# K~ by pairs, h in two parts, rows from two engines and the scan's profiled durations in a planned attention and feed-forward kernel

## The chip, the cores and the metric

The kernel runs on one core of one Trainium2 chip. The metric is device microseconds of one execution. A run of each kernel consists of several timed executions and one profiled one; where ratios are given, they are the mean time of one kernel's fast runs over the mean time of the other's fast runs of the same rounds, so they are not quite the ratio of the medians that are quoted beside them.

## The reference

Two blocks follow each other. The first is a gated linear recurrence with a complex decay; the second is a feed-forward layer with a squared relu. Cut to what matters:

```python
# q, k, v, a_re, a_im: (batch 4, heads 8, seq 768, head_dim 48), fp32
a = (a_re, a_im) * min(|a|, 0.999) / (|a| + 1e-6)
for t in range(S):                      # S complex, 48 x 48 per head
    S = a[t] * S  (complex)
    S.re += outer(k[t], v[t])
    y[t] = q[t] @ S.re
x = y, heads side by side               # 3072 tokens x 384
h = x @ w_in                            # 384 -> 2048
out = maximum(h, 0) ** 2 @ w_out        # 2048 -> 384
```

## The kernel before

The work is cut into 8 units: 4 batches times 2 halves of 384 rows. In each unit VectorE computes running products of the decay (the "scan", which leaves them in `e` and `x`), TensorE transposes them back (`tot`, `bk`), multiplies them into q and k (`P`, only in units 0 and 1, the "early" ones), and goes through four pairs of heads: `tq` transposes, `sa` scores, `kv` states, `ypair` the mix of both. Each pair's result `yt` is moved by DMA into the rows `xT`. Then come 16 products `h` (768 matmul records for all units, 0.32 us each, two for each matmul call) and the products `o`. Weights arrive as raw words and VectorE converts them (`w`), with ScalarE's help (`lower`, tile `raw`).

The program sets the order on every engine. The kernel registers steps with an engine, a planned cost, a lag, a rank and dependencies, and a small list scheduler lays them out once, while the program is built:

```python
step(key, engine, cost, rank, deps, fn, lag=None, bank=None, until=None)

def lay_out():                          # cut
    while ready:
        # for every engine: the earliest ready step, rank breaks near ties
        ...
        free[engine] = t + cost         # the plan's clock, not the chip's
        done[key] = t + cost + lag
```

So a planned cost changes no work; it moves the place of later steps in an engine's list. The parts that the change touches:

```python
# the scan's planned cost (10 parts on VectorE in every unit)
sizes = [96] * 3 + [48, 45, 42, 36, 24, 45]
costs = [dve_cost(2 * m, 2 * m, m, m) for m in sizes] + [dve_cost(*[279] * 6)]
# dve_cost(*ns) is the sum of 80 + int(1.04 * n)
...
def rows(z, i):         # K~ through memory, half a unit (2 pairs, 576 KB) at a time
    if i == 0:
        nc.gpsimd.dma_start(out=<rows in memory>, in_=<all of u["K", z]>)
    else:
        nc.gpsimd.dma_start(out=<KC>, in_=<rows in memory, read another way>)
...
def place():            # a pair's rows of xT
    for h in range(2):
        ...
            nc.sync.dma_start(out=u["xT"][...], in_=u["yt", i][...])
...
def hidden(f):          # one block of h
    ps = u["h", f] = dp.tile([C, L], F32, name="h", tag="d")
    for m in range(NM):                 # NM = 3
        nc.tensor.matmul(ps, lhsT=w1[:, f, m], rhs=u["xT"][:, m], ...)
...
step(("h", n, f), "PE", 1940, ..., [("xT", n, i) for i in range(NP)] + ...)
```

## Time and profile before

| | before |
|---|---|
| time, median of 3 | 777.3 us (776.74 to 778.57) |
| span of the profiled execution | 776.3 us |
| h of unit 0 starts | 90.27 us |
| unit 1's scan ends on VectorE | 155.3 us |
| h of unit 1 starts | 191.85 us |
| from there to the end | 584.45 us |

The last two rows cut the span in two: a first part, in which the early units start up, and a second part, in which the units follow each other.

GpSimd's order of time (start, duration, engine, line, transfer; in brackets what it waited for before):

```profile
72.51 1.52 POOL L658 DMA_DIRECT2D raw<-in_moe_w_in_dram  x2 [3.46 <-DVE w L683]
74.03 0.76 POOL L1100 DMA_DIRECT2D KC<-rows  x1
```

The read back stands behind two weight fetches, which wait for VectorE.

### The profile page before, as it was taken

Reading aid. Unit: us, or ns where it says so; the run is one execution under the profiler, and the core shown is the slowest. Engines: PE = TensorE matmul, PEld = TensorE weight load, DVE = VectorE, ACT = ScalarE, POOL = GpSimd, SP = SyncE. Lnnn points to the kernel's source line nnn. Section 1 sums busy time; section 2 is a strip of 40 time slices with the busy share of each in tenths; the row PEclk is TensorE's granted clock in tenths of the full one; section 3 lists DMA queues with packets and bytes.
Section 4 is the critical chain, followed back from the end, with each engine's and each line's share of the span. In section 5 each row is a group of like instructions: output and inputs, shape, how many; then the busy total and the mean of one; then the engine's idle time right before and its main releaser. Section 6 shows DMA issues by size and latency. Waiting matters only on the chain.

```text
span 776.3 us, 9918 instructions
## 1 busy us (share of the span) xinstructions
PE 709.7 (91%) x3538; PEld 474.8 (61%) x3538; DVE 503.3 (65%) x1184; ACT 409.8 (53%) x754; POOL 107.2 (14%) x157
## 2 busy tenths in 40 slices
PE   0249699998899999999999999999999999999997
PEld 0138555577568657766866676676577555555553
DVE  4789888879796797769667988967954660000000
ACT  5638187346868538772867378686154303502510
POOL 5002100031031103102110401310022420000000
PEclk9999699999899999999999999999999999999999
DMA  9517462043134207203520522331052870000000
GB/s 278 168 30 238 141 206 77 21 154 109 35 118 141 58 20 230 54 3 111 176 51 1 178 82 56 125 121 38 15 193 90 292 238 11 2 11 21 0 11 24
DMA packets 39067, 76.24 MB, mean 98 GB/s; under 512 B 10752, under 2 KB 25216, under 8 KB 39008
## 3 DMA queue, kind: packets, MB, share of 16 engines
q0 software_dynamic: 14208, 53.88, 21.7%
q1 hardware_dynamic: 24800, 21.64, 9.2%
q8 instruction: 30, 0.49, 0.3%
q14 instruction: 29, 0.24, 0.1%
HBM read 56.62 MB, written 14.16 MB: 91 GB/s over the span
## 4 chain that ended last, share of the span: by engine, by line
PE 68%; DVE 21%; ACT 3%; DMA 3%; issue 2%; SPq 0%; POOL 0%; ACTq 0%; DVEq 0%
PE h L1280 24%; PE o L1297 23%; DVE fa L982 5%; PE sa L1186 5%; PE tq L1173 4%; PE kv L1200 3%; PE ypair L1222 3%; DVE e L989 3%; PE P L1081 2%; PE ypair L1227 2%; DMA KC<-rows 2%; DVE fa L987 1%; ACT fa L808 1%; DVE e L990 1%; DMA xT<-yt 1%
## 5 line engine op out<-in xcount | busy, mean ns | idle before, releaser
L1280 PE MATMUL h<-xT,w 128*128 128x384 f32 x768 | 261.1, 495 | 6.5 <-DMA xT<-yt 6.5
L1297 PE MATMUL o<-w,g 128*128 128x384 f32 x768 | 254.5, 487 | 0.0
L1280 PEld LDWEIGHTS h<-xT,w 128*128 128x128 f32 x768 | 144.9, 193 | 101.4 <-issue 8.4
L1297 PEld LDWEIGHTS o<-w,g 128*128 128x128 f32 x768 | 143.5, 190 | 94.1 <-issue 0.7
L1287 ACT ACTIVATE g<-h 128x384 f32<-128x384 f32 x128 | 62.5, 488 | 93.4 <-PE h L1280 93.3
L1178 ACT COPY QKT<-tq 96x512 f32<-96x512 f32 x96 | 76.2, 871 | 34.2 <-PE tq L1173 33.5
L1302 ACT COPY ot<-o 128x384 f32<-128x384 f32 x24 | 11.5, 479 | 122.9 <-PE o L1297 121.3
L1290 ACT ACTIVATE g<-g 128x384 f32<-128x384 f32 x128 | 67.0, 523 | 3.5
L1186 PE MATMUL sa<-QKT 96*128 96x128 f32 x384 | 53.8, 282 | 1.5 <-ACT QKT L1178 0.9
L1186 PEld LDWEIGHTS sa<-QKT 96*128 96x128 f32 x384 | 47.7, 191 | 7.9 <-ACT QKT L1178 1.9
L1173 PE MATMUL tq<-ident,QK 128*96 128x128 f32 x384 | 50.8, 273 | 0.4 <-DVE QK L1087 0.4
L1192 DVE TENSOR_TENSOR A<-sa,mask 128x384 f32<-128x384 f32 x64 | 35.2, 552 | 22.5 <-PE sa L1186 21.6
L982 DVE TENSOR_TENSOR fa<-e 128x192 f32<-128x192 f32 (+6 forms) x152 | 48.3, 358 | 2.0
L1173 PEld LDWEIGHTS tq<-ident,QK 128*96 128x96 f32 x384 | 42.4, 126 | 10.2 <-issue 6.4
L808 ACT ACTIVATE fa<-fb 128x576 f32<-128x576 f32 x64 | 41.3, 675 | 6.3 <-DVE fb L816 3.5
L935 PE MATMUL tot<-ident,last 128*128 128x128 f32 x72 | 12.6, 306 | 31.1 <-ACT last L861 27.3
L805 DVE TENSOR_TENSOR fb<-fa 128x576 f32<-128x576 f32 x32 | 24.1, 755 | 25.8 <-ACT fa L800 13.6
L1222 PE MATMUL ypair<-A,v 128*48 128x128 f32 x384 | 37.7, 287 | 2.4 <-ACT yt L1232 1.9
L762 POOL DMA_DIRECT2D a<-in_a_re_dram x12 | 9.0, 753 | 209.3 <-issue 99.3
L1200 PE MATMUL kv<-v,KC 128*96 128x48 f32 x320 | 32.7, 254 | 2.9 <-DMA KC<-rows 2.9
L1200 PEld LDWEIGHTS kv<-v,KC 128*96 128x96 f32 x320 | 31.7, 173 | 5.5 <-DMA KC<-rows 2.8
L1087 DVE TENSOR_TENSOR QK<-qk,fa 128x576 f32<-128x576 f32 x48 | 33.1, 755 | 0.0
(105 smaller groups left out, 828.6 us busy)
## 6 DMA issues: line engine op xcount, KB each, us to landing
rows<-QK POOLq DMA_DIRECT2D x16, 576.0 KB, 4.0
raw<-in_moe_w_in_dram POOLq DMA_DIRECT2D x16, 384.0 KB, 7.7
raw<-in_moe_w_out_dram SPq DMA_DIRECT2D x16, 384.0 KB, 3.7
look<-in_moe_w_in_dram POOLq DMA_DIRECT2D x16, 384.0 KB, 4.6
look<-in_moe_w_out_dram POOLq DMA_DIRECT2D x16, 384.0 KB, 4.6
KC<-rows POOLq DMA_DIRECT2D x8, 576.0 KB, 5.4
out_dram<-ot SPq DMA_DIRECT2D x24, 192.0 KB, 1.9
xT<-yt SPq DMA_DIRECT2D x48, 72.0 KB, 2.8
```

The costliest lines, as they stand in the source:

```text
L808: act.activation(out=parts(z)[dst], in_=parts(z)[src], func=func, **kw)
L982: dve.tensor_tensor(out=t, in0=x, in1=y[:, j].unsqueeze(1).to_broadcast(shape), op=ALU.mult)
L1173: nc.tensor.transpose(ps[:, 2 * j + h], src, ident)
L1178: act.copy(out=u["T", i].rearrange("r z (p c) -> r c z p", c=W)[:, c], in_=u["tq", i, c])
L1186: nc.tensor.matmul(sa[:, j], lhsT=T[:, 2 + h, ts(j, C)], rhs=T[:, h, ts(j, C)], start=True, stop=True)
L1192: dve.tensor_tensor(out=u["A", i][:, h], in0=u["sa", i, h], in1=mask3, op=ALU.mult)
L1200: nc.tensor.matmul(ps[:, j, h], lhsT=u["KC", hh // HH][:, j, hh % HH], rhs=u["v"][:, j, hh], start=True, stop=True)
L1222: nc.tensor.matmul(ypair[64 * h:64 * h + D, ts(j, C)], lhsT=u["v"][:, j, 2 * i + h], rhs=A[:, h, j], start=True, stop=S_j is None)
L1280: nc.tensor.matmul(ps, lhsT=w1[:, f, m], rhs=u["xT"][:, m], start=(m == 0), stop=(m == NM - 1))
L1287: act.activation(out=t, in_=u["h", f], func=AF.Relu)
L1290: act.activation(out=u["g", f], in_=u["g", f], func=AF.Square)
L1297: nc.tensor.matmul(u["o", c], lhsT=u["g", f][:, ts(c, C)], rhs=w2[:, f], start=(f == 0), stop=(f == NF - 1))
```

## The change

Its intent has four parts: in units 0 and 1 send K~ through memory pair by pair, with the last product stage `P` ordered by pairs too; split the first three blocks of h so that two thirds of each need no last rows of xT; let ScalarE issue half of the last rows in those units; and give the plan the scan's durations as profiled. One more edit comes with it: the q and k loads of unit 1 are now planned behind the last read back of K~ of unit 0. (Some planned lags and ranks move too: of the first `a` loads, of the K~ transfers, of the rows and of h.) Cut to its core:

```diff
@@ loads
-                        if name == "a" else [("ap", n - 1, z)],
+                        if name == "a" else [("ap", n - 1, z)]
+                        + ([("KC", 0, 1, NP - 1)] if n == 1 else []),
@@ scan
-        sizes = [96] * 3 + [48, 45, 42, 36, 24, 45]
-        costs = [dve_cost(2 * m, 2 * m, m, m) for m in sizes] + [dve_cost(*[279] * 6)]
+        costs = [1475] * 3 + [1010, 980, 940, 880, 760, 970, 2300]
@@ K~ through memory
+        def pairs_of(z):
+            of_z = range(z * NP // 2, (z + 1) * NP // 2)
+            return list(of_z) if early else [of_z]
...
+            for i in pairs_of(z):
+                ... one "rows" and one "KC" transfer for each entry
@@ the last rows of xT
+        def aside(h):
+            return n < 2 and i == NP - 1 and h == 1
...
+                (nc.scalar if aside(h) else nc.sync).dma_start(
@@ h in two parts
+            apart = f < BANKS["d"]
+            if apart:
+                step(("h0", n, f), "PE", 1290, ..., lambda f=f: hidden(f, range(NM - 1)), ...)
+            step(("h", n, f), "PE", 650 if apart else 1940, ...
+                 lambda f=f, apart=apart: hidden(f, [NM - 1] if apart else range(NM)), ...)
```

More of the change, by code (lines that the diff above doesn't have):

```diff
@@ L775, in chain_steps @@
                         [("f", n - 1, z, i, r) for i in range(2) for r in range(2)]
-                        if name == "a" else [("ap", n - 1, z)],
+                        if name == "a" else [("ap", n - 1, z)]
+                        + ([("KC", 0, 1, NP - 1)] if n == 1 else []),
                         lambda name=name, z=z, j=j: load(name, z, j),
-                        lag=(3300 + 1500 * z if name == "a" else 8000) if n == 0 else 6000)
+                        lag=(3300 + 2500 * z if name == "a" else 8000) if n == 0 else 6000)
         for j in range(W):
@@ L1088, in apply, with rows @@
                               in0=u["qk", z][:, j, hi], in1=p, op=ALU.mult)
-        def rows(z, i):
-            if i == 0:
+        def rows(z, i, back):
+            if ("rows", z) not in u:
                 u["rows", z] = dram.tile([L, HH * R], F32, name="rows", tag=f"rows{z}")
+            m = HH // len(pairs_of(z)) * R
+            e = slice(i % (HH * R // m) * m, (i % (HH * R // m) + 1) * m)
+            if not back:
                 nc.gpsimd.dma_start(
-                    out=u["rows", z].rearrange("(p c) e -> p (c e)", c=W),
-                    in_=u["K", z].rearrange("p c h e -> p (c h e)"))
-            else:
-                kc = u["KC", z] = nat.tile([C, NM, HH, R], F32, name="KC", tag=f"KC{z}")
-                m = NM - u["half"]
-                nc.gpsimd.dma_start(
-                    out=kc[:, 0:m].rearrange("p j h e -> p j (h e)"),
-                    in_=u["rows", z].rearrange("(j p) e -> p j e", p=C)[:, 0:m])
+                    out=u["rows", z].rearrange("(p c) e -> p c e", c=W)[:, :, e],
+                    in_=u["K", z].rearrange("p c h e -> p c (h e)")[:, :, e])
+                return
+            if ("KC", z) not in u:
+                u["KC", z] = nat.tile([C, NM, HH, R], F32, name="KC", tag=f"KC{z}")
+            j = NM - u["half"]
+            nc.gpsimd.dma_start(
+                out=u["KC", z][:, 0:j].rearrange("p j h e -> p j (h e)")[:, :, e],
+                in_=u["rows", z].rearrange("(j p) e -> p j e", p=C)[:, 0:j, e])
+        def pairs_of(z):
+            of_z = range(z * NP // 2, (z + 1) * NP // 2)
+            return list(of_z) if early else [of_z]
         for z in range(2):
@@ L1106, in chain_steps @@
             was_read = [("tq", n - 1, i, c) for i in of_z for c in range(W)] + [
-                ("rows", n - 1, z)]
+                ("rows", n - 1, z, i) for i in of_z]
             add(("ov", n, z), "DVE", D1, [("xn", n, 2), ("rest", n, z), ("kk", n, z)],
@@ L1114, in chain_steps @@
             done = []
-            for r in range(2):
-                made = [("f", n, z, 0, r), ("f", n, z, 1, 1 - r)]
-                if early:
-                    for i in range(2):
-                        P = ("P", n, z, r, i)
-                        qk = [("QK", n, z, j, r, i) for j in (1, 0)]
-                        add(P, "PE", 970, made + [("ov", n, z)] + was_read, lambda z=z, r=r, i=i: join_pe(z, r, i),
-                            rank=-3000 if z == 0 else -1950 + 40 * n, bank="sc", until=qk[1])
-                        for j, key in zip((1, 0), qk):
-                            add(key, "DVE", 410, [P, qk[0] if j == 0 else P], lambda z=z, j=j, r=r, i=i: apply(z, j, r, i))
-                            done.append(key)
-                else:
-                    add(("join", n, z, r), "DVE", D1, made,
-                        lambda z=z, r=r: join(z, r))
+            for i, r in ((i, r) for i in range(2) for r in range(2)) if early else ():
+                P = ("P", n, z, r, i)
+                qk = [("QK", n, z, j, r, i) for j in (1, 0)]
+                add(P, "PE", 970, [("f", n, z, 0, r), ("f", n, z, 1, 1 - r), ("ov", n, z)]
+                    + was_read, lambda z=z, r=r, i=i: join_pe(z, r, i),
+                    rank=-3000 if z == 0 else -1950 + 40 * n, bank="sc", until=qk[1])
+                for j, key in zip((1, 0), qk):
+                    add(key, "DVE", 410, [P, qk[0] if j == 0 else P],
+                        lambda z=z, j=j, r=r, i=i: apply(z, j, r, i))
+                    done.append(key)
+            for r in () if early else range(2):
+                add(("join", n, z, r), "DVE", D1, [("f", n, z, 0, r), ("f", n, z, 1, 1 - r)],
+                    lambda z=z, r=r: join(z, r))
             if not early:
@@ L1136, in chain_steps @@
             add(("ap", n, z), "DVE", 0, done, lambda: None)
-            for i, (name, lag) in enumerate((("rows", 4800), ("KC", 5200))):
-                add((name, n, z), "POOL", 750,
-                    [x for x in done if x[3] == 1] + [("rows", n, z) if i else ("KC", n - 1, z)]
-                    + ([("kv", n - 1, x) for x in of_z] if i else []),
-                    lambda z=z, i=i: rows(z, i), rank=-100, lag=lag)
+            for i in pairs_of(z):
+                whole_z = not early
+                keys = [x for x in done if x[3] == 1 and (whole_z or x[5] == i % 2)]
+                pairs = of_z if whole_z else [i]
+                for name, lag, deps in (
+                        ("rows", 4800 if whole_z else 3800,
+                         keys + [("KC", n - 1, z, x) for x in of_z]),
+                        ("KC", 5200 if whole_z else 4200,
+                         [("rows", n, z, pairs[0])] + [("kv", n - 1, x) for x in of_z])):
+                    add((name, n, z, pairs[0]), "POOL", 750, deps,
+                        lambda z=z, i=pairs[0], name=name: rows(z, i, name == "KC"),
+                        rank=-100, lag=lag)
+                    for x in pairs[1:]:
+                        add((name, n, z, x), "POOL", 0, [(name, n, z, pairs[0])],
+                            lambda: None)
     carry = {}
@@ L1232, in mixed, with place, pieces @@
             act.copy(out=u["yt", i][0:64 + D], in_=ypair[0:64 + D])
-        def place():
+        def place(h):
             if "xT" not in u:
                 u["xT"] = xp.tile([C, NM, L], F32, name="xT", tag="xT")
-            for h in range(2):
-                r, end = (2 * i + h) * D, (2 * i + h + 1) * D
-                p = 64 * h
-                while r < end:
-                    m = min(end - r, C - r % C)
-                    nc.sync.dma_start(out=u["xT"][r % C:r % C + m, r // C],
-                                      in_=u["yt", i][p:p + m])
-                    r, p = r + m, p + m
+            for r, p, m in pieces(h):
+                (nc.scalar if aside(h) else nc.sync).dma_start(
+                    out=u["xT"][r % C:r % C + m, r // C], in_=u["yt", i][p:p + m])
+        def pieces(h):
+            r, end, p = (2 * i + h) * D, (2 * i + h + 1) * D, 64 * h
+            while r < end:
+                m = min(end - r, C - r % C)
+                yield r, p, m
+                r, p = r + m, p + m
+        def aside(h):
+            return n < 2 and i == NP - 1 and h == 1
         rank = -2000 + 10 * x
@@ L1250, in pair_steps @@
         for c in range(W):
-            step(("tq", n, i, c), "PE", 430, rank + c, [("ap", n, z)] + free, lambda c=c: turn(c),
+            step(("tq", n, i, c), "PE", 430, rank + c,
+                 ([("QK", n, z, j, r, i % 2) for j in range(2) for r in range(2)]
+                  if n < 2 else [("ap", n, z)]) + free, lambda c=c: turn(c),
                  bank=bank(c == 1), until=("T", n, i, c))
@@ L1262, in pair_steps @@
         step(("kv", n, i), "PE", 330 * chunks, rank + 4,
-             [("KC", n, z), ("v", n, W - 1), ("mix", n - 1, NP - 1)] + free, keep, bank=bank(True), until=("S", n, i, chunks - 1))
+             [("KC", n, z, i), ("v", n, W - 1), ("mix", n - 1, NP - 1)] + free, keep, bank=bank(True), until=("S", n, i, chunks - 1))
         for j in range(chunks):
@@ L1269, in pair_steps, with hidden @@
              [("A", n, i, h) for h in range(2)] + [("S", n, i, chunks - 1), was("y", 1)], mix)
-        step(("y", n, i), "ACT", 400, -25, [("mix", n, i), was("xT", 2)], mixed)
-        step(("xT", n, i), "SP", 600 * (3 if i % 4 in (1, 2) else 2), -25, [("y", n, i), ("h", n - 2, NF - 1)], place, lag=2400)
+        step(("y", n, i), "ACT", 400, -25, [("mix", n, i)] + [was("xT", 2, h) for h in range(2)],
+             mixed)
+        for h in range(2):
+            step(("xT", n, i, h), "ACT" if aside(h) else "SP", 600 * len(list(pieces(h))), -24,
+                 [("y", n, i), ("h", n - 2, NF - 1)], lambda h=h: place(h), lag=2400)
     def dense_steps(u):
         n = u["n"]
-        def hidden(f):
-            ps = u["h", f] = dp.tile([C, L], F32, name="h", tag="d")
-            for m in range(NM):
-                nc.tensor.matmul(ps, lhsT=w1[:, f, m], rhs=u["xT"][:, m],
+        def hidden(f, ms):
+            if ms[0] == 0:
+                u["h", f] = dp.tile([C, L], F32, name="h", tag="d")
+            for m in ms:
+                nc.tensor.matmul(u["h", f], lhsT=w1[:, f, m], rhs=u["xT"][:, m],
                                  start=(m == 0), stop=(m == NM - 1))
@@ L1310, in dense_steps @@
             room = [("o", n - 1, W - 1, f // 4), ("fetch", NF - 1),
-                    ("cv", (list(range(3, 8)) + list(range(FIRST, NF)))[f // 2], 2)]
-            step(("h", n, f), "PE", 1940, 1000 * n + f,
-                 [("xT", n, i) for i in range(NP)] + [("cv", f, 2), ("h", n, f - 1)] + room,
-                 lambda f=f: hidden(f), bank="d", until=("relu", n, f))
+                    ("cv", (list(range(3, NF // 2)) + list(range(FIRST, NF)))[f // 2], 2)]
+            apart = f < BANKS["d"]
+            if apart:
+                step(("h0", n, f), "PE", 1290, 1000 * n + f,
+                     [("xT", n, i, h) for i in range(NP - 1) for h in range(2)]
+                     + [("cv", f, 2), ("h0", n, f - 1), ("kv", n, NP - 1)] + room
+                     + [("tq", n, NP - 1, c) for c in range(W)],
+                     lambda f=f: hidden(f, range(NM - 1)), bank="d", until=("relu", n, f))
+            step(("h", n, f), "PE", 650 if apart else 1940, 1000 * n + 20 + f,
+                 [("xT", n, i, h) for i in range(NP) for h in range(2)]
+                 + [("h0", n, f) if apart else ("cv", f, 2), ("h", n, f - 1)] + room,
+                 lambda f=f, apart=apart: hidden(f, [NM - 1] if apart else range(NM)),
+                 bank=None if apart else "d", until=("relu", n, f))
             step(("relu", n, f), "ACT", 420, -17, [("h", n, f)],
```

## The prediction

> **What bounds the kernel now.** I read the page first, then TensorE's waits, then busy time by stretch, then the order of instructions around each long wait.
>
> The page says 776.3 us of span, of which TensorE is busy for 91%:
>
> ```profile
> PE 709.7 (91%) x3538; PEld 474.8 (61%) x3538; DVE 503.3 (65%) x1184; ACT 409.8 (53%) x754; POOL 107.2 (14%) x157
> PE   0249699998899999999999999999999999999997
> ```
>
> So TensorE is the bound, except at the start, and the change can only win where TensorE is idle or slow. TensorE's waits (total, times, longest):
>
> ```profile
> PE tot L935 <- ACT last L861: 27.3, 1, 27.3
> PE bk L935 <- DVE e L989: 14.0, 6, 11.7
> PE h L1280 <- DMA xT<-yt: 6.5, 2, 3.6
> ...
> PE kv L1200 <- DMA KC<-rows: 2.9, 2, 2.3
> PE ypair L1222 <- ACT yt L1232: 1.9, 2, 1.3
> ```
>
> The first two rows are almost wholly the first chain before 50 us, which the change leaves as it is. The next rows lie at the end of units 0 and 1. TensorE's order of time there, with the wait ahead of each group in brackets:
>
> ```profile
> 80.97 4.07 PE L1200 MATMUL kv<-v,KC 128*96 128x48 f32 x24 [2.28 <-DMA KC<-rows]
> ...
> 96.15 4.22 PE L1280 MATMUL h<-xT,w 128*128 128x384 f32 x7 [2.95 <-DMA xT<-yt]
> ```
> ```profile
> 196.98 1.62 PE L1280 MATMUL h<-xT,w 128*128 128x384 f32 x2 [3.57 <-DMA xT<-yt]
> ```
>
> Busy time by stretch shows a second cost behind each wait; the column PEclk is the granted clock:
>
> ```profile
> 79.50:93.20 13.70, 11.61 (x68) 8.90 (x68) 10.36 (x29) 1.51 (x3) 2.68 (x3) 0.50 0.26 68
> 93.20:96.60 3.40, 0.45 (x2) 0.32 (x3) 3.40 (x9) 0.00 (x0) 0.00 (x0) 1.00 0.98 291
> 96.60:100.00 3.40, 3.40 (x7) 1.89 (x6) 2.06 (x5) 2.02 (x4) 0.00 (x0) 0.50 0.99 360
> ...
> 195.60:202.40 6.80, 5.42 (x13) 3.53 (x14) 3.69 (x6) 5.46 (x11) 0.00 (x0) 0.50 0.23 59
> ```
>
> Work done at half clock costs half of its time: (11.61 + 3.40 + 5.42)/2 = 10.2 us. The waits from 57 to 202 us add up to about 12.7 us (0.94, 2.28, 0.62, 2.95, 1.27, 0.50, 3.57 and crumbs). So 22.9 us is the most that the change can win.
>
> [...] For 576 KB [...] the trace has 4.0 median for rows<-QK and 5.4 for KC<-rows[...]. [...] An xT issue takes 0.58 us here, so ScalarE's help is worth 0.6 us at each of two places. [...] the read back must wait for the write's completion. GpSimd does wait here, 26.1 us in 8 times.
>
> **The change part by part.** *K~ by pair.* Before, the last K~ product (68.5) starts a 576 KB write; its read back is issued only at 74.03, behind two weight fetches that wait for VectorE, and lands at 80.9. After, pair 2 is written at about 65.0, read at 68 and lands near 72; its kv is wanted near 75. Pair 3 is still behind the two fetches in GpSimd's order, but with half the bytes; I put its landing at 78.5. TensorE's order has sa, mix and tq of pair 2 in front of it, so kv of pair 3 is wanted near 80. The price: kv of pairs 0 and 1 (2.2 us) now stands ahead of the last P, so that product ends near 70.3 instead of 68.5. Counting TensorE on from there at full clock, h of unit 0 starts at about 83 instead of 90.27, and no clock loss precedes it.
>
> *h in two parts.* In the trace an h product is two matmul records of 0.323 us, so 0.645 us. Now six products (two of the three parts of three blocks, as many as there are banks) need no last xT rows: 3.9 us of work, where before two (1.3 us) went ahead. The last rows come about 4 us after the last mix. So both waits shrink from 2.95 and 3.57 to 0 to 0.7, and the clock stays up: for unit 1 that alone is 3.57 + 5.42/2 = 6.3 us.
>
> *What of unit 0's 12 us arrives.* When o of unit 0 begins, TensorE would be ahead by 7.3 (h starts sooner) + 2.95 (xT wait) + 1.5 (half of the 2.93 us of h at half clock before 93.2) + 1.7 (half of 3.4 after 96.6) - 0.8 (a remaining xT wait) = about 12.6 us. But unit 1's attention starts when VectorE has unit 1's scan, and VectorE is nearly full:
>
> ```profile
> 68.50:155.20 86.70, 79.85 (x354) 51.96 (x353) 75.67 (x192) 48.99 (x95) 6.27 (x8) 0.90 0.39 125
> ```
>
> VectorE was busy 75.67 of 86.70 us. Its waits there:
>
> ```profile
> DVE St L1212 <- PE kv L1200: 3.2, 2, 2.1
> DVE w L683 <- ACT raw L665: 2.5, 2, 1.3
> DVE fb L813 <- ACT fa L808: 1.8, 1, 1.8
> DVE fb L805 <- ACT fa L903: 1.3, 2, 1.0
> ```
>
> The first two rows (5.7 us) stem from late kv and late relus and go away; the other two are the chain itself and stay. Less 0.4 to 1 us for the later last product, unit 1's scan ends about 4.7 us earlier: 155.2 becomes 150.5. TensorE's order in the new kernel puts all of o before P of unit 1, so TensorE idles some 3 to 4 us there, and its clock may drop once more (estimate 1.2 us).
>
> From the scan, P can start after two qk products (1.36 us for both) and two fa/fb products (0.67 each), some 2.8 us later, at 153.3. Before, P to h took 191.85 - 158.35 = 33.5 us, of which 2.58 were o (8 matmuls, now done earlier) and 2.1 waits: 28.8 us of work. With 1.5 us of waits and 1.2 us of clock loss, h of unit 1 starts at 153.3 + 31.5 = 184.8, 7.0 us sooner.
>
> *The scan's durations* change no work. They move the read backs, the transposes of e and the loads of unit 1's q and k in the order; q and k now queue ahead of the last xT rows on SyncE.
>
> *Sum.* From h of unit 1 on, TensorE is full and the order has enough h ahead of the next unit's e (42 h products instead of 27), so the gain stays: 7.0 + 6.3 - 0.4 (a remaining xT wait) - 0.5 (order) = 12.4 us. Span 776.3 - 12.4 = 763.9; runs read 1.0 us above the profile's span (777.3), so 765.
>
> **The rivals.** *VectorE holds everything:* kv of pairs 0 and 1 waits for memory, and the last P, in order behind it, comes 2 us later; that shifts VectorE's whole list. For: write and read take 9.3 us before (57.9 to 67.2) and would have 9.1 us after. Against: q and k of unit 1, 576 KB, no longer compete there. Time then 768 to 770. *DMA traffic eats the xT gain:* four q and k loads (1.15 MB), three v loads and the fetches stand in front of the last rows; before, they landed 4.6 us after issue. For: the DMA share is 0.98 in 93 to 97 us. Against: ScalarE's half goes by its own queue, and 3.9 us of h cover it. Time then 767. *All goes through:* VectorE loses nothing, TensorE's clock holds at the start of unit 1, and h of unit 1 starts at 182.4. Time then 761 to 762. *Nothing gained, all swallowed by VectorE:* only the xT wait and the clock of unit 1 remain, 6.3 us, time 771.
>
> **Range and chances.** The first three rivals put the spread at 761 to 770; I widen it to 759 to 771, as waits that an order by hand misses are more often added than removed. 2% is 761.8, which only the best rival reaches: 0.24. Slower by 2% would need new waits of 28 us: 0.01.
>
> **What would show it.** Right: kv waits of unit 0 under 1 us and full clock from 57 us to the end of h of unit 0; h of unit 0 starting at 82 to 85 with six products before any xT wait; VectorE's waits for kv and raw gone; unit 1's scan ending at 149.5 to 151.5; a TensorE wait of 2 to 4 us for e or fa before P of unit 1; h of unit 1 starting at 183 to 186 and no half clock after it. Wrong: kv of pair 1 or pair 3 waiting 2 us or more; half clock in unit 0; the scan of unit 1 not before 154; or waits for e in units 2 to 6 above the 2 us or so of before.

## The result, and the profile after

The changed kernel takes 767.3 us (median of 4, 765.82 to 767.91) against 777.93 us (median of 4) in the same rounds. The ratio is 0.986, 95% interval 0.9835 to 0.9884. The prediction was 765.0 with a range of 759 to 771, and "within 2%" was the likeliest class, so it was right in range and in class.

The cut of the span tells a different story from the sum:

| | before | predicted | after |
|---|---|---|---|
| h of unit 0 starts | 90.27 | about 83 | 81.88 |
| unit 1's scan ends | 155.3 | 150.5 | 155.9 |
| h of unit 1 starts | 191.85 | 184.8 | 188.91 |
| from there to the end | 584.45 | 579.1 | 576.2 |
| span | 776.3 | 763.9 | 765.1 |

("579.1" is 763.9 less 184.8.) The first part gave 2.9 us instead of 7.0, the second 8.3 instead of 5.4. The two errors nearly cancelled. These are the figures of one profile of each kernel: a second profile of the changed kernel (e10 below) cuts at 187.16 us and has 575.3 from there, so each of the two differences is known to 1 or 2 us only.

The page: busy time and share of each engine, then TensorE's busy share and its granted clock in tenths, in 40 slices.

```profile
PE 701.0 (92%) x3538; PEld 469.1 (61%) x3538; DVE 505.7 (66%) x1184; ACT 408.6 (53%) x754; POOL 114.4 (15%) x165
...
PE   0249699989999999999999999999999999999996
...
PEclk9999899999999999999999999999999999999999
```

TensorE does the same number of matmuls in 8.7 us less busy time. That is the half clock: it cost 10.2 us before (the prediction's sum) and costs 3.13/2 = 1.6 us now, as the stretches below show. (In before a group of four `ypair` records is followed by the next after 0.22 us at 69.85 us, where the granted clock is 1.00, and after 0.43 us at 85.85 us, where it is 0.50.) The dip that is left in the clock row is at the fifth slice, in unit 0. TensorE's waits (total, times, longest):

```profile
PE tot L936 <- ACT last L862: 27.7, 2, 26.7
PE bk L936 <- DVE e L990: 12.3, 2, 11.7
PE h L1309 <- DMA xT<-yt: 6.9, 2, 5.8
...
PE P L1081 <- DVE fa L1068: 2.7, 2, 1.4
...
PE kv L1217 <- DMA KC<-rows: 0.2, 1, 0.2
```

The kv wait went from 2.9 to 0.2 us, and the wait for e from 14.0 in 6 times to 12.3 in 2. But the wait for xT, which the split was to remove, rose from 6.5 to 6.9. TensorE's order of time shows where, first for unit 0, then for unit 1:

```profile
81.88 4.14 PE L1309 MATMUL h<-xT,w 128*128 128x384 f32 x12
91.86 28.86 PE L1309 MATMUL h<-xT,w 128*128 128x384 f32 x84 [5.85 <-DMA xT<-yt]
...
188.91 4.14 PE L1309 MATMUL h<-xT,w 128*128 128x384 f32 x12
194.08 6.04 PE L1309 MATMUL h<-xT,w 128*128 128x384 f32 x18 [1.04 <-DMA xT<-yt]
```

The six early products (12 records, 4.14 us) run before both waits, as planned. In unit 1 that leaves 1.04 us of wait. In unit 0 it leaves 5.85 us, and from 88 to 95 us the granted clock is 0.51. Busy time by stretch (us; busy and count of PE, PEld, DVE, ACT, POOL; PEclk; DMA share; GB/s):

```profile
57.00:88.00 31.00, 28.69 (x249) 23.54 (x247) 28.79 (x74) 18.54 (x30) 10.19 (x13) 1.00 0.66 197
88.00:95.00 7.00, 3.13 (x5) 1.85 (x6) 6.40 (x16) 0.69 (x2) 0.00 (x0) 0.51 1.00 333
95.00:200.00 105.00, 99.01 (x481) 65.05 (x480) 87.35 (x198) 67.53 (x128) 14.49 (x19) 1.00 0.33 101
```

Full clock from 57 to 88 us is what the prediction wanted. From 88 to 95 us the clock is half and the DMA share is 1.00. That share alone does not say that transfers hold TensorE (in e1 below it reads 1.07 in the same stretch, and TensorE is busy throughout); the wait of 5.85 us for xT does. Which transfers stand around those of xT is in the order of time of all engines (only the issues are shown):

```profile
...
81.22 0.58 SPq L762 DMA_DIRECT2D qk<-in_q_dram  x1
...
81.84 0.51 SPq L762 DMA_DIRECT2D qk<-in_k_dram  x1
...
82.30 2.68 POOL L768 DMA_DIRECT2D v<-in_v_dram  x3 [7.15 <-DMA xT<-yt]
82.45 0.45 SPq L762 DMA_DIRECT2D qk<-in_q_dram  x1
82.63 0.67 ACTq L1256 DMA_DIRECT2D xT<-yt  x1
...
82.94 0.75 SPq L762 DMA_DIRECT2D qk<-in_k_dram  x1
...
83.79 0.52 SPq L1256 DMA_DIRECT2D xT<-yt  x1
...
```

Four loads of 288 KB stand directly ahead of the last 72 KB of xT on SyncE's queue; three v loads of 192 KB start beside them, and ScalarE's half of the rows. The issues of 81 to 93 us with their size and median time to landing:

```profile
v<-in_v_dram POOLq DMA_DIRECT2D x3, 192.0 KB, 6.9
xT<-yt ACTq DMA_DIRECT2D x1, 72.0 KB, 5.8
xT<-yt SPq DMA_DIRECT2D x1, 72.0 KB, 7.9
```

The late rows delay more than TensorE. They delay the relus of h on ScalarE, in whose list the next `lower` of a raw weight stands behind them; and VectorE's list stands at the conversion of that weight. ScalarE's and VectorE's order of time:

```profile
93.52 0.49 ACT L1316 ACTIVATE g<-h 128x384 f32<-128x384 f32 x1 [10.92 <-PE h L1309]
...
98.50 0.53 ACT L665 ACTIVATE raw<-raw 128x384 uint32<-128x384 uint32 x1
...
99.06 0.56 DVE L683 CUSTOM_DVE_ANT_0 w<-raw,w 128x768 uint16<-128x768 uint16 x1 [4.60 <-ACT raw L665]
```

VectorE's wait for raw was 2.5 us before and is 6.0 us in two times now. It removed its wait for kv (3.2 us) and bought this one. So unit 1's scan ends where it ended before, and what TensorE had won up to h of unit 0 was lost to it.

The second part shows no such event. Here is the stretch from 215 to 640 us, for before and then for after:

```profile
215.00:640.00 425.00, 421.77 (x2335) 289.39 (x2334) 326.84 (x752) 247.90 (x451) 77.08 (x109) 1.00 0.34 109
```
```profile
215.00:640.00 425.00, 423.50 (x2344) 291.60 (x2344) 327.52 (x748) 245.25 (x445) 77.62 (x109) 1.00 0.35 110
```

TensorE idles 3.23 us of these 425 before and 1.50 us after. More of the 8.3 us lies in unit 1: 2.5 us less wait for xT, and the half clock of 195.6 to 202.4 us, worth 5.42/2 = 2.7 us, is gone. That is 6.9 us (1.7 + 2.5 + 2.7); some 1.3 us are spread over busy time and I cannot assign them.

At this point the split looked like the carrier of the second part, and the q and k loads like the thief of the first.

### The profile page after: what moved, and what is told of

The parts are those of the page before. It is cut to its first block, busy times and chain, and to the rows that moved or that the text cites. A ratio compares the mean times of both kernels' runs of the same rounds, so it can differ in the third digit from the quotient of the medians.

```text
span 765.1 us, 9919 instructions
## 1 busy us (share of the span) xinstructions
PE 701.0 (92%) x3538; PEld 469.1 (61%) x3538; DVE 505.7 (66%) x1184; ACT 408.6 (53%) x754; POOL 114.4 (15%) x165
## 4 chain that ended last, share of the span: by engine, by line
PE 77%; DVE 12%; ACT 3%; DMA 3%; issue 2%; SPq 0%; POOL 0%; DVEq 0%; ACTq 0%
PE h L1309 30%; PE o L1326 27%; PE sa L1203 5%; PE tq L1190 5%; PE kv L1217 3%; PE ypair L1239 3%; DMA xT<-yt 2%; PE ypair L1244 2%; DVE fa L983 2%; PE P L1081 1%; ACT fa L809 1%; DVE QK L1087 1%; DMA KC<-rows 1%; PE tot L936 1%; PE bk L936 1%
## 5 line engine op out<-in xcount | busy, mean ns | idle before, releaser
L1309 PE MATMUL h<-xT,w 128*128 128x384 f32 x768 | 257.7, 489 | 6.9 <-DMA xT<-yt 6.9
L1309 PEld LDWEIGHTS h<-xT,w 128*128 128x128 f32 x768 | 143.4, 191 | 100.2 <-issue 10.2
L1190 PEld LDWEIGHTS tq<-ident,QK 128*96 128x96 f32 x384 | 42.6, 126 | 10.2 <-issue 6.7
L936 PE MATMUL tot<-ident,last 128*128 128x128 f32 x72 | 12.3, 295 | 31.5 <-ACT last L862 27.7
L843 DVE TENSOR_TENSOR fa<-a 128x384 f32<-128x384 f32 x64 | 32.5, 551 | 0.4
L768 POOL DMA_DIRECT2D v<-in_v_dram x18 | 16.0, 894 | 107.2 <-PE ypair L1244 100.1
## 6 DMA issues: line engine op xcount, KB each, us to landing
rows<-QK POOLq DMA_DIRECT2D x12, 576.0 KB, 3.5
```

The costliest lines, as they stand in the source:

```text
L1190: nc.tensor.transpose(ps[:, 2 * j + h], src, ident)
L1309: nc.tensor.matmul(u["h", f], lhsT=w1[:, f, m], rhs=u["xT"][:, m], start=(m == 0), stop=(m == NM - 1))
```

## The experiments

Twelve runs, all with 5 rounds. "First" is the start of h of unit 1 and "second" is from there to the end of the profiled execution.

| run | median us | ratio to before (95%) | span | first | second |
|---|---|---|---|---|---|
| the kernel before | 777.93 | 1 | 776.3 | 191.85 | 584.5 |
| the changed kernel | 767.30 | 0.9860 (0.9835 to 0.9884) | 765.1 | 188.91 | 576.2 |
| e10, changed kernel again | 768.13 | 0.9873 (0.9852 to 0.9895) | 762.5 | 187.16 | 575.3 |
| e1, q and k behind the rows | 762.45 | 0.9829 (0.9796 to 0.9863) | 759.6 | 182.67 | 576.9 |
| e11, the same again | 763.20 | 0.9804 (0.9779 to 0.9828) | 761.5 | 183.94 | 577.6 |
| e2, q and k early | 765.01 | 0.9864 (0.9830 to 0.9899) | 761.2 | 183.90 | 577.3 |
| e3, v behind the rows | 769.42 | 0.9922 (0.9887 to 0.9956) | 764.1 | 187.34 | 576.8 |
| e4, q, k and v behind | 761.36 | 0.9808 (0.9774 to 0.9843) | 761.6 | 183.77 | 577.8 |
| e5, h not split | 766.03 | 0.9893 (0.9870 to 0.9916) | 763.3 | 186.50 | 576.8 |
| e6, K~ by half units | 767.48 | 0.9896 (0.9877 to 0.9915) | 765.8 | 189.76 | 576.0 |
| e7, all rows by SyncE | 766.56 | 0.9885 (0.9862 to 0.9908) | 764.4 | 187.18 | 577.2 |
| e8, old durations | 776.94 | 1.0029 (1.0010 to 1.0048) | 774.2 | 187.62 | 586.6 |
| e9, before + new durations | 772.50 | 0.9922 (0.9899 to 0.9946) | 770.4 | 191.06 | 579.3 |
| e12, e1 without the split | 764.25 | 0.9825 (0.9799 to 0.9851) | 763.1 | 184.67 | 578.4 |

The medians of before were 776.55 (call of e1 to e4), 775.33 (e5 to e8) and 777.55 (e9 to e12), and single executions of before ran from 772.21 to 779.41, so ratios are to be preferred to medians, and differences under 2 us between calls are not to be trusted.

### What holds the last rows of xT in unit 0

The theory was that the q and k loads, moved by the change to just ahead of the rows, cause the 5.85 us; the rival was the v loads and the traffic as a whole.

e1 only moves the loads behind the rows in SyncE's list; the lists of TensorE, ScalarE and GpSimd stay the same, VectorE's differs a little.

```diff
-                        + ([("KC", 0, 1, NP - 1)] if n == 1 else []),
+                        + ([("xT", 0, NP - 1, h) for h in range(2)] if n == 1 else []),
```

> The changed kernel with one edit: the four q and k loads of unit 1 are queued on SyncE behind the last xT rows of unit 0 instead of ahead of them; the order of TensorE and GpSimd is the same. Theory 1 (those 1.15 MB[...] are what makes h of unit 0 wait 5.85 us): the wait falls to 2.5 us or less, the half clock from 88 to 95 us is gone or shorter, VectorE's wait for raw (6.0 us in 2 times) goes back to about 2 to 3, unit 1's scan ends at 151 to 153 instead of 155.6, and the time is 762 to 765. Theory 2 (the v loads on GpSimd's queue and the weight fetches, so the DMA traffic as a whole, do it): the wait stays at 4 us or more, the scan of unit 1 ends after 154.5 and the time is 766 to 768.

TensorE's order of time in e1, and its busy time in the stretch where the changed kernel was at half clock:

```profile
81.73 4.14 PE L1309 MATMUL h<-xT,w 128*128 128x384 f32 x12
87.07 27.33 PE L1309 MATMUL h<-xT,w 128*128 128x384 f32 x84 [1.21 <-DMA xT<-yt]
```
```profile
88.00:95.00 7.00, 7.00 (x23) 4.10 (x22) 6.93 (x18) 5.88 (x13) 0.00 (x0) 1.00 1.07 376
```

The wait falls from 5.85 to 1.21 us, with the clock full, although the v loads still start at 82.15 us. The rows now land 4.4 and 4.6 us after issue instead of 7.9 and 5.8. VectorE's wait for raw falls from 6.0 to 0.2 us, below the 2 to 3 us that were expected, and unit 1's scan ends at 149.7 us, earlier than the expected 151 to 153:

```profile
DVE fb L814 <- ACT fa L809: 2.1, 1, 2.1
...
DVE w L683 <- ACT raw L665: 0.2, 1, 0.2
```

h of unit 1 starts at 182.67 us. Theory 1 holds: the q and k loads are enough to cause most of the wait.

e2 takes the new dependency away, so that the loads go out early as they did before, among the K~ transfers.

```diff
-                        + ([("KC", 0, 1, NP - 1)] if n == 1 else []),
+                        ,
```

> The changed kernel with one edit: the q and k loads of unit 1 are issued as early as before (between 58 and 69 us), when K~ goes through memory. Theory 1: the xT wait of unit 0 falls to 2.5 us or less as in the run with the loads behind the rows, but the loads now meet the K~ writes and reads, so the landing of KC<-rows goes from 4.1 us median towards 5 and kv of unit 0 waits 1 us or more in sum; time 763 to 766. Theory 2: the xT wait stays at 4 us or more, and with the kv wait on top the time is 767 to 770.

The xT wait is 1.2 us here too, KC<-rows lands after 4.7 us median against 4.1 in e1, and kv waits for KC 1.5 us in two times. The time is 765.01, within theory 1's range. h of unit 0 starts at 83.03 in e2 against 81.73 in e1, so the change's new dependency may have freed the K~ transfers by 1.3 us; but e3 below, whose lists are the changed kernel's up to there, starts it at 84.66, so a difference of that size between two profiles is not proof. Timed, e2 equals the changed kernel (0.9864 against 0.9860 and 0.9873): a gain of the new dependency over the old place of the loads does not show.

e3 and e4 were to move the v loads, with one more dependency:

```diff
-                + ([("e2", 0, 1)] if n == 1 else []),
+                + ([("e2", 0, 1)] if n == 1 else []) + ([("xT", 0, NP - 1, h) for h in range(2)] if n == 2 else []),
```

e3 has it alone, e4 together with the edit of e1.

> The changed kernel with one edit: the three v loads of unit 2 (0.59 MB, GpSimd's queue) wait for the last xT rows of unit 0; the q and k loads stay ahead of the rows. Theory 1: the xT wait falls by less than 2 us (from 5.85 to 4 or more)[...]; time 765 to 767.5. Theory 2: the wait falls by 2.5 us or more, to about 3, and the time to 763 to 765.

> The changed kernel with both edits: the q and k loads and the v loads are behind the last xT rows of unit 0. Both theories let the xT wait of unit 0 fall to 1 us or less and the clock stay full. What it tells apart is how much of the time that wait is worth: if VectorE's list is held by the late relus, unit 1's scan ends at 150 to 152 and the time is 761 to 763; if VectorE is held by something else, the scan still ends after 154, TensorE waits longer ahead of P of unit 1, and the time is 765.5 to 767.5, the same as the changed kernel.

The edit did not do what it was meant to do. The trace of e3 shows the first v load and the last rows:

```profile
84.87 1.32 POOL L768 DMA_DIRECT2D v<-in_v_dram  x1 [8.28 <-issue]
85.32 0.52 SPq L1256 DMA_DIRECT2D xT<-yt  x1
85.32 0.60 ACTq L1256 DMA_DIRECT2D xT<-yt  x1
```

The v loads start 0.45 us ahead of the rows, not behind them. In e4 they start at 81.94 us and the rows at 82.18; in the changed kernel it was 82.30 and, for ScalarE's half, 82.63. The dependency counts in the plan only. GpSimd's list has the same order in all of these runs, and no wait on the chip came of it. So neither run tests what the v loads do.

e3 up to 98 us has the lists of the changed kernel, and so it shows scatter: kv waits 1.36 us for KC, h of unit 0 starts at 84.66, 2.8 us later, the rows are issued 1.9 us after the last q or k issue and not 0.1, and they land after 3.4 and 4.8 us. The wait ahead of the third part of h is 0.38 us. This suggests that the loads hold the rows the less, the longer a start they have; two executions do not prove it. Its time, 769.42 (765.95 to 773.29), fits neither theory, and it spreads more than that of any other run. e4 is in effect e1 again, up to some 94 us: the same xT wait (1.2 us), P of unit 1 at the same time (151.56 against 151.73), 761.36 us.

So a share of the v loads in the wait is neither shown nor excluded. That the q and k loads are enough to cause most of it is shown by e1 and e2, where the v loads start 0.2 us ahead of ScalarE's rows, as before, and the wait is 1.2 us.

e10 and e11 put the changed kernel and e1 beside each other on one chip, unedited:

> The changed kernel again, unedited, as the measure for the other runs of this call and for the scatter between profiles of one program: time 766 to 768, h of unit 1 at 187 to 189 us, 576 to 578 us from there to the end, the xT wait of unit 0 between 4 and 6 us.

> The changed kernel with the q and k loads of unit 1 behind the last xT rows, again, beside the changed kernel itself: 762 to 763, so 4 to 5 us faster than the changed kernel in the same rounds, h of unit 1 at 182 to 184 us. If the difference seen in the first call was scatter, the two agree within 2 us.

768.13 against 763.20 us; the ratios 0.9873 and 0.9804 differ by 0.0069, or 5.4 us of 777.55. The intervals do not overlap. The collision thus costs about 5 us, of which the first part shows 3.2 in this pair of profiles (187.16 against 183.94) and 6.2 when the first profiles of both are compared (188.91 against 182.67). The clock makes part of this difference: P of unit 1 starts at 151.72 us in e11 and at 151.73 in e1, but e11 then has half clock from 152.2 to 155.6 us (two P records take 1.17 us there and 0.65 to 0.75 after it), and its h of unit 1 starts 1.3 us later. (The prediction had put such a loss at 1.2 us.) e10 also shows the scatter: its xT wait is 4.26 us and not 5.85, its span is 2.6 us shorter, and its second part, 575.3, is below what was expected.

### The parts of the change, taken away one by one

e5 takes the split away from the changed kernel:

```diff
-            apart = f < BANKS["d"]
+            apart = False
```

> The changed kernel without h in two parts (each block of h waits for all xT rows, as before). If the split is worth what the prediction says, 3.9 us of work no longer stand ahead of each xT wait and at most 1.3 us do: the waits for xT grow by 2 to 3 us each (unit 0 from 5.85 to about 8, unit 1 from 1.04 to about 3.5), and half clock comes back at h of unit 1 (6.8 us at half, 2 to 3 us of loss): time 771 to 775. If VectorE swallows what happens in unit 0, only unit 1's part remains: 769 to 772.

Both expectations failed: 766.03 us, by the ratios 1.6 to 2.6 us behind the changed kernel's two runs. The waits for xT did come back, 6.47 us in unit 0 and 3.19 us in unit 1. In unit 0 VectorE sets the start of unit 1 in any case. In unit 1 two things repaid the wait. TensorE idles only 0.09 us from 215 to 640 us instead of 1.50. And the half clock did not come back: TensorE's clock is 1.00 from 185 to 203 us, although the wait is nearly that of before (3.57). The traces show how much work stood around the two waits. Half clock begins at 195.58 us in before; here are the 3.41 us ahead of it, and two stretches of the same length over which the wait of e5 is spread:

```profile
192.17:195.58 3.41, 1.24 (x4) 0.38 (x2) 2.45 (x7) 2.04 (x3) 2.66 (x3) 1.00 0.38 100
```
```profile
186.20:189.61 3.41, 1.86 (x10) 0.79 (x6) 3.31 (x7) 0.58 (x2) 2.66 (x3) 1.00 0.33 79
189.61:193.02 3.41, 1.76 (x6) 1.13 (x7) 3.34 (x7) 2.45 (x5) 0.00 (x0) 1.00 0.58 138
```

In before 1.24 us of matmul work lie in that stretch, and half clock follows. In e5 there are 1.86 and 1.76 us, and the clock stays at 1.00. What decides between the two was not shown. Leaving out the split is not enough to keep the clock up: in e12 below, also without the split, it fell.

e12 asks the same of e1, where nothing stands ahead of the rows:

```diff
-            apart = f < BANKS["d"]
+            apart = False
```

> The changed kernel with the q and k loads behind the rows and without h in two parts, to see what the split is worth once nothing stands in front of the rows. If it is worth its 2.6 us of covered wait at each place: the xT waits are about 4 us (unit 0) and 3.2 us (unit 1) instead of 1.2 and 0.8, and the time is 4 to 6 us above the run with the split, 766 to 769. If VectorE sets P of unit 1 anyway and the order gives back the rest, as in the run without the split before: 762 to 764.

TensorE's order of time in unit 0:

```profile
82.81 1.56 PE L1309 MATMUL h<-xT,w 128*128 128x384 f32 x4
88.17 12.19 PE L1309 MATMUL h<-xT,w 128*128 128x384 f32 x32 [3.81 <-DMA xT<-yt]
```

The waits are those of the first expectation (3.81 and 3.45 us), and here half clock comes with both, for 3.4 us each (from 88.06 and 190.46 us; the granted clock is 0.76 from 88 to 95 us and 0.94 from 191.06 to 215). Yet the time is nearly that of the second: 764.25 against 763.20 us. TensorE does not idle from 215 to 640 us, where in e11 it idles 2.96 us. The ratios differ by 0.0021, or 1.6 us, and the intervals overlap. So the split is worth some 2 us, not 6.3.

e6 sends K~ of the early units through memory by half units again:

```diff
-            return list(of_z) if early else [of_z]
+            return [of_z]
...
-                whole_z = not early
+                whole_z = True
```

> The changed kernel with K~ of units 0 and 1 through memory by half a unit as before (the last product stage still goes by pairs). If the pairs are what lets h of unit 0 start at 81.9 us with full clock, the wait of kv for KC comes back (2 us or more), half clock comes back between 79 and 93, and h of unit 0 starts at 87 to 90. If unit 1's scan is bound by VectorE and not by this, the time is nearly unchanged (767 to 769); if the gain of the unit 0 part reaches the end, it is 772 to 776.

The kv wait is back (1.6 us), h of unit 0 starts at 90.03 us, and the clock is half again:

```profile
79.50:93.20 13.70, 11.86 (x69) 9.59 (x70) 11.12 (x30) 1.50 (x3) 2.95 (x3) 0.51 0.61 172
```

Yet P of unit 1 starts at 156.92 us, between the two profiles of the changed kernel (157.98, and 156.23 in e10), and the time is 767.48 us, by the ratios 1.8 to 2.8 us behind the changed kernel's two runs, with intervals that overlap. In e6 the q and k loads go out from 76 to 79 us and the last rows only at 90.69, and TensorE does not wait for xT in unit 0; so VectorE waits 2.4 us for kv and only 0.2 us for raw; in the changed kernel it is 0 and 6.0 (4.6 in e10). Most of the 8 us by which the pairs bring h of unit 0 forward is lost again to the collision that they run into. With the loads out of the way (e1) P of unit 1 starts 5.2 us earlier than in e6 (151.73).

e7 gives all rows back to SyncE:

```diff
-            return n < 2 and i == NP - 1 and h == 1
+            return False
```

> The changed kernel with all xT rows issued by SyncE, as before. The prediction valued ScalarE's share at one issue, 0.6 us, at each of two places. If it is no more than issue time, the xT waits grow by 0.5 to 1 us each and the time is 768 to 769; if ScalarE's queue also lets half of the rows pass the q and k loads, the wait of unit 0 grows by 2 us or more and the time is 769 to 771; if the q and k loads hold the other half anyway, nothing changes (767 to 767.8).

766.56 us, and the xT waits are 3.88 and 0.68 us, no longer than with ScalarE's help. By the ratio e7 is 0.9 to 1.9 us behind the changed kernel's two runs, but the intervals overlap. It is the third expectation, if a little below its range; the prediction's 0.6 us at each of two places can be neither seen in the waits nor ruled out by the time. In the changed kernel the half of the rows on ScalarE's queue still took 5.8 us to land beside the loads.

e8 gives the plan the scan's old durations:

```diff
-        costs = [1475] * 3 + [1010, 980, 940, 880, 760, 970, 2300]
+        sizes = [96] * 3 + [48, 45, 42, 36, 24, 45]
+        costs = [dve_cost(2 * m, 2 * m, m, m) for m in sizes] + [dve_cost(*[279] * 6)]
```

> The changed kernel with the scan's old durations in the plan. No work changes, only order. The prediction gave this part 0: time 766.5 to 768.5 and the same waits to 1 us. If the new durations carry part of the gain, the time is 769 to 772, and the waits of VectorE or TensorE in units 1 to 6 show where.

This is the miss that matters. The time is 776.94 us, ratio 1.0029: the whole gain is gone, more than either expectation allowed. And it is not lost in the first part, where e8 is as fast as e10 (187.62 against 187.16); up to 155 us no engine's list differs. It is lost in the second: 586.6 us, 10 us above the changed kernel and even 2 above before. TensorE's waits from 200 to 640 us, and its busy time:

```profile
PE bk L936 <- DVE e L990: 6.9, 6, 1.5
...
```
```profile
215.00:640.00 425.00, 416.56 (x2316) 285.94 (x2315) 324.04 (x744) 243.06 (x442) 77.26 (x109) 1.00 0.34 109
```

TensorE idles 8.44 us there instead of 1.50. From h of unit 1 to the end it idles 16.4 us instead of 8.5; the remaining 2.5 us of the difference lie in busy time. One of the six places, in e8:

```profile
265.86 0.49 PE L936 MATMUL bk<-ident,x 128*128 128x128 f32 x3
266.19 7.91 PE L1327 MATMUL o<-w,g 128*128 128x384 f32 x24
275.18 0.97 PE L936 MATMUL bk<-ident,e 128*128 128x128 f32 x6 [1.09 <-DVE e L990]
```

and the same place in the changed kernel:

```profile
271.19 0.49 PE L936 MATMUL bk<-ident,x 128*128 128x128 f32 x3
271.52 5.33 PE L1326 MATMUL o<-w,g 128*128 128x384 f32 x16
276.68 5.97 PE L1309 MATMUL h<-xT,w 128*128 128x384 f32 x18
282.49 0.82 PE L936 MATMUL bk<-ident,e 128*128 128x128 f32 x6
```

Between the transpose of x and that of e the list has 24 records (7.9 us) with the old durations and 34 records (11.3 us) with the new ones. The scan needs the longer time. Its old planned cost is the sum of its parts: 2.75 us for the first three, 3.40 for the next six and 2.22 for the last, 8.4 us; the new one is 12.3 us. In the trace the ten parts of unit 1 take from 143.46 to 155.92 us, 12.5 us, in the changed kernel (one of the first three 1.5 us, for instance 144.98 to 146.49), so the new figure is the true one. The old plan believed e to be ready 3.9 us too early and put TensorE in front of it.

e9 is the other side: the kernel before with the new durations and nothing else.

```diff
-        sizes = [96] * 3 + [48, 45, 42, 36, 24, 45]
-        costs = [dve_cost(2 * m, 2 * m, m, m) for m in sizes] + [dve_cost(*[279] * 6)]
+        costs = [1475] * 3 + [1010, 980, 940, 880, 760, 970, 2300]
```

> The kernel before with one edit: the scan's durations in the plan as profiled; no pairs, no split, all rows by SyncE, q and k loads where they were. Theory A (the durations carry the second part of the gain, because the plan had put the transposes of e some 4 us too early in TensorE's list in every unit): h of unit 1 starts near 191 to 192 as before, but from there to the end it takes 577 to 580 us instead of 584.5, TensorE's waits for e after 60 us fall from 2.3 us to 0.5 or less, time 769 to 773. Theory B (the prediction's: durations are worth 0 and the split of h carries the second part): 584 us from h of unit 1 to the end, time 775 to 778.

Theory A holds. The first part is unchanged (191.06), the second takes 579.3 us, and the wait for e after 60 us is gone. From 215 to 640 us TensorE does not idle at all:

```profile
191.06:215.00 23.94, 20.49 (x63) 12.13 (x63) 18.29 (x56) 18.00 (x35) 2.67 (x3) 0.86 0.14 34
215.00:640.00 425.00, 425.00 (x2352) 293.17 (x2351) 322.38 (x729) 248.22 (x451) 76.34 (x107) 1.00 0.34 106
```

The time is 772.50 us, ratio 0.9922: one edit that changes no work gains 6 us alone, where the whole change gains 10 (e10).

## Why the prediction was right or wrong

The number was right, and its steps were so only in part; that two errors of opposite sign nearly cancelled was luck. Two of the prediction's own signs of being wrong came: half clock in unit 0 (from 88.1 to 95.0 us), and the scan of unit 1 not before 154 us.

**K~ by pair up to h of unit 0: right.** kv of pair 3 was wanted near 80 us and came at 79.2 without a wait; h started at 81.88 where about 83 was predicted; the clock was full (1.00 from 57 to 88 us). The halved pieces landed after 3.3 and 4.1 us (e1) where whole ones took 4.0 and 5.4 (before), 0.7 and 1.3 us less.

**"The last rows come about 4 us after the last mix. So both waits shrink from 2.95 and 3.57 to 0 to 0.7": wrong for unit 0.** Unit 1 kept 1.04 us. In unit 0 the wait was 5.85 us. The rival "DMA traffic eats the xT gain" had named the very loads, and the prediction even says that they "now queue ahead of the last xT rows on SyncE"; but it rated the loss at 2 us, to 767, and let 3.9 us of h cover it. The median was indeed 767.3, but the path there was not this rival's: the loss at the rows was larger, and the durations made up for it. The rows came 4.8 us later than in e1 (h goes on at 91.86 and not at 87.07): 3.5 us because SyncE's half took 7.9 us to land instead of 4.4, the rest because it was issued behind the loads' issues. e1 and e11 remove this cause alone.

**"The first two rows (5.7 us) stem from late kv and late relus and go away": half wrong.** The kv row went. The raw row grew from 2.5 to 6.0 us, since late rows make late relus, and ScalarE's `lower` stands behind a relu. Unit 1's scan ended at 155.9 and not at 150.5. In e1 both rows are gone, the scan ends at 149.7, and h of unit 1 starts at 182.67 and, in e11, at 183.94; predicted was 184.8. So the chain of the first part was understood; its one wrong term was the xT wait of unit 0, 0.8 in the sum and 5.85 on the chip, and VectorE passed it on.

**"For unit 1 that alone is 3.57 + 5.42/2 = 6.3 us": wrong.** The wait did shrink and the half clock did go, as the profile of after shows. But the 6.3 us are not what the split is worth. Without it (e5) the wait is 3.19 us, the half clock is gone nevertheless, and the second part takes 576.8 us against 576.2. One cause is the clock: half clock came with a wait of 3.4 to 3.5 us in e9 (0.86 over 191 to 215 us) and in e12 (0.94 there), and not with one of 3.2 us in e5 (1.00 from 185 to 203 us); why was not shown. The other is that the split's order has idle time further on, 1.5 us in the changed kernel and 3.0 in e11, where e5 and e12 have 0.1 and none. Together the split is worth some 2 us.

**"The scan's durations change no work": true, and the conclusion "0" wrong.** The prediction listed what they move, the transposes of e among them, and gave that no price, because TensorE's waits for e after 60 us came to only 2.3 us. They were the largest part: 6 us alone (e9), and without them the other parts together give nothing (e8). The parts do not add up: what the durations carry depends on the list that they are laid out with.

**The sum.** Too much by 4.1 us in the first part, too little by 2.9 in the second: 12.4 predicted, 11.2 measured in the profiled spans. The median reads 2.2 us above the profiled span (767.3 against 765.1); the prediction took 1.0. Each execution reads 1.7 to 1.8 us above its own span (766.86 against 765.1 for the profiled one after, 778.07 against 776.3 before): the 1.0 came from comparing a median with the span of an execution slower than it.

What stays open: what the v loads add to the wait for the rows, and what decides whether half clock comes with a wait. Then: with the old durations the changed kernel idles 8.44 us between 215 and 640 us where before idles 3.23, though their plans are wrong by the same 3.9 us. The lists differ (before has 16 matmul calls between the transposes in two units where e8 has 12), but I did not find which edit tips them. Also some 1 to 2 us of the second part's gain, in e9 as in the changed kernel, lie in busy time that I could not assign.

The experiments give a faster kernel: the changed one with the q and k loads of unit 1 behind the last rows, 763.20 us against 768.13 in the same rounds.

## What to carry to other kernels

Where a plan lays out the instructions, check each planned duration against the trace before touching the structure: a cost that was 3.9 us short in every unit gave 6 us alone, and the rest of this change added 4 to it as it stood (e10) and 9 with the q and k loads behind the rows (e11). When a change moves a load to a later place to free one transfer, look which small, urgent transfer now stands behind it in the same queue (here 72 KB on SyncE's queue landed after 7.9 us behind 1.15 MB of loads, and after 4.4 us ahead of them, in e1). And price a part by taking it away alone; what two profiles show beside each other (here the wait and the half clock of unit 1) need not belong to the part that was meant to do it. Last, look in the trace whether an edit moved what it was to move, before reading its time.
